# Score and value matmuls woven into one another, and matmuls that run on weights already loaded

## The chip, the cores and the metric

The kernel runs on one core of one Trainium2 chip. Its time is the device time of one execution in microseconds (us); the figure given is the median of several executions, and one more execution is profiled. TensorE (PE in the profile) does the matmuls; a weight load (LDWEIGHTS, PEld) puts the stationary operand into its array, and a matmul streams the other operand through. VectorE (DVE) and ScalarE (ACT) read the results, which stand in eight banks of PSUM, GpSimd (POOL) does some sums, and SyncE (SP) issues most DMAs.

## The reference

Two attention blocks read the same x of 2048 x 1024 (bfloat16) and are mixed by a gate per row. A is linear attention, B a local one over 8 positions, 2 apart, back from each row's own. Both have 32 heads of 32.

```python
x = A_x
g = sigmoid((x * gate_w).sum(-1, keepdims=True))

# A: linear attention
q, k, v = split(x @ A_wqkv)
phi = lambda t: where(t > 0, t + 1, exp(t)) + 1e-6
kv = einsum("bhsd,bhse->bhde", phi(k), v)
z = phi(k).sum over s
a = (phi(q) @ kv) / (phi(q) . z + 1e-6) @ A_wo

# B: position s sees s, s-2, ..., s-14
q, k, v = split(x @ B_wqkv)
logits = (q . k[s - 2 w]) / sqrt(32), masked where s - 2 w < 0
b = (softmax(logits) @ v[s - 2 w]) @ B_wo

out = g * a + (1 - g) * b
```

## The kernel before

Rows are reordered so that even positions come first and odd ones second: B's window is then 8 neighbours within one half. There are 16 tiles of 128 rows; xT holds x transposed, tile by tile. The program is a list of operations, each with an engine, a cost, what it reads and writes, and a function that emits its instructions (`P.op`). A planner (`Prog.schedule`) runs through that list with the costs, gives each engine its order, and lets free operations go to VectorE or ScalarE, whichever the plan has free first; PSUM banks come from pools, and the plan is made six times, each time with the banks' release times of the one before. Semaphores are put where an operation needs another engine's result. An operation of TensorE is one unit: its waits stand ahead of its first instruction, its signal on its last.

The stages on TensorE, in order:

1. Fifty small matmuls on constant ones (L1399, `WARM`), 156 columns each, while the first data comes.
2. B's values (L1363 by `group`): for each tile of x and each half (512 columns) of the weights eight matmuls of 128x512 add up in one bank; a move (L1390, L1391, `vst`) takes it out, and a DMA stores it in HBM (`vB_hbm`). The list `steps` sets the order: in a block of four tiles first the four with the first half, then the four with the second. Some steps carry an early load of later weights (`early`).
3. B's keys and queries (kT, qT; L1363), 64 groups of eight matmuls.
4. A's keys with phi (L1363), then the product of x and those keys (pk, xn; L1707). Every fifth group or so a burst of B's attention stands between them (`fill` and `burst`).
5. A's state (L1685), queries of A (kT, xT; L1363), folds of the state into the output weights (L1733), a flag of one column (L1621, `all_ok`) that says whether the fast path is valid, and the output products (L1778), 16 tiles by two halves, with each tile's normalized queries transposed into aT by DMA (L1763).

A burst has two parts. The scores (L1513): for each of 8 chunks four matmuls of 64x64 weights and 114 columns, one in each quadrant of the array. The values (L1537) of the burst before: for each of 16 head pairs four matmuls of 64x57 weights (the exponentials E) and 33 columns (v). There are 18 fills; the first burst has scores alone, the last values alone, and 17 have both. Before the change a burst emits all scores, then all values:

```python
            def fn(e):
                last = s_fn(e) if s_fn else None
                return v_fn(e) if v_fn else last
```

ScalarE's exponential (L1518) and VectorE's division (L1548, L1549) wait for the burst's signal. In all stages each matmul comes with its own weight load.

Of the kernel before, what the change touches and what calls it, by code (L numbers as in the profile page):

```python
# [1119 lines left out]
def build_kernel(nc, A_x, A_wqkv, A_wo, B_x, B_wqkv, B_wo, gate_w, out):  # L1120
    del B_x
    S = A_x.shape[1]
# [59 lines left out]
    banks = [Bank(i) for i in range(8)]  # L1182
# [14 lines left out]
    ws = [SB([128, 8, 1024], BF16, "w%d" % i) for i in range(4)]  # L1197
# [62 lines left out]
    def plan(seen):  # L1260
# [97 lines left out]

        def group(bank, lhs, rhs, reads, lo=0, hi=8):
            def fn(e):  # L1360
                last = None
                for dc in range(lo, hi):
                    last = e.matmul(bank.ap(), lhs(dc), rhs(dc), start=(dc == 0), stop=(dc == 7))  # L1363
                return last
            return P.op("pe", fn, (hi - lo) * mm(512), reads=reads, writes=[bank.iv])
# [32 lines left out]
        for i in range(WARM):  # L1398
            P.op("pe", lambda e: e.matmul(banks[7].ap(0, 156), one(128), one(156), start=True, stop=True), 0.13, writes=[banks[7].iv], prio=-1)  # L1399
# [4 lines left out]
        steps = []  # L1404
        for b in range(NT // 4):
            for half in range(2):
                if b == 0:
                    cuts = [(0, 4), (4, 6), (6, 8)] if half == 0 else [(0, 2), (2, 4), (4, 6), (6, 8)]
                    steps += [[(i, half, lo, hi) for i in range(2)] for lo, hi in cuts]
                    steps += [[(2, half, 0, 8)], [(3, half, 0, 8)]]  # L1410
                else:
                    steps += [[(4 * b + i, half, 0, 8)] for i in range(4)]
# [71 lines left out]
        def burst(s_fn, reads, cost):  # L1484
# [13 lines left out]
        def fill(e_, qs, nq, offs):  # L1498
# [10 lines left out]
            def s_fn(e):  # L1509
                for c in range(8):  # L1510
# [4 lines left out]
                return last  # L1515
# [13 lines left out]
            def v_fn(e):  # L1529
                for i in range(16):  # L1530
# [8 lines left out]
                return last  # L1539
# [365 lines left out]
```

## Time and profile before

| | |
|---|---|
| median of 3 runs | 479.21 us (479.09 to 479.43) |
| the profiled execution's own time | 479.6 us |
| its span | 477.9 us |
| granted TensorE clock, mean | 0.998 |
| TensorE busy | 468.0 us, 3988 matmuls in the records, 4035 weight loads |
| VectorE busy | 316.5 us |
| ScalarE busy | 130.0 us |

The span reaches from the first to the last instruction of the program; the execution's time is 1.7 us longer. Some matmul records are missing from the trace, so distances between matmuls that are twice the usual one are a missing record and no pause. A matmul's record is longer than its share of the time, since matmuls overlap: the distance from one start to the next is what it costs. The engine names are those above; in a group's row stand the line, the engine, the operation, what it writes and reads, the shape, the count, then busy time and mean length, then the idle time ahead of it.

### The profile page before, as it was taken

The page shows a single profiled execution, that of the slowest core. Times are in us where ns is not written, and L with a number is a line of the kernel's source. Part 1 is how long each engine was busy: PE and PEld are TensorE (multiplying, and loading weights), DVE is VectorE, ACT ScalarE, POOL GpSimd, SP SyncE. Part 2 cuts the span into 40 slices and gives each one's busy share as a digit, 9 for nine tenths or more (in the row PEclk, how much of TensorE's full clock was granted, in tenths as well). Part 3 has the DMA queues.
Part 4 walks back from the last instruction along what each step waited for, and adds up shares of the span by engine and source line. Part 5 has one row for each costly group of instructions (what it writes and reads, how often), then busy time and mean ns, then how long its engine had stood idle before and what let it go on. Part 6 is the DMA issues. An engine that isn't in the chain of part 4 may idle for free.

```text
span 477.9 us, 9322 instructions
## 1 busy us (share of the span) xinstructions
PE 468.0 (98%) x3988; PEld 226.1 (47%) x4035; DVE 316.5 (66%) x555; ACT 130.0 (27%) x174; POOL 40.2 (8%) x39
## 2 busy tenths in 40 slices
PE   9999999999999999999999999999999999999996
PEld 6444444444445444454445445544444444444444
DVE  2121276799877788878865465599987777777512
ACT  1112121112243535555543423153211111111000
POOL 3000000000000000000068551100000000000000
PEclk9999999999999999999999999999999999999999
DMA  9999995132211253354325876771241111421111
GB/s 234 229 214 315 355 363 153 59 118 67 67 37 51 67 167 85 80 158 124 77 71 154 182 166 128 152 207 45 68 88 45 44 46 50 73 55 45 46 44 48
DMA packets 94969, 57.07 MB, mean 119 GB/s; under 512 B 55240, under 2 KB 88392, under 8 KB 94920
## 3 DMA queue, kind: packets, MB, share of 16 engines
q1 hardware_dynamic: 94088, 55.61, 43.6%
q10 hardware_dynamic: 832, 0.79, 0.7%
q8 instruction: 33, 0.54, 0.5%
q14 instruction: 16, 0.13, 0.1%
HBM read 30.56 MB, written 12.72 MB: 91 GB/s over the span
## 4 chain that ended last, share of the span: by engine, by line
PE 98%; issue 1%; DVE 0%
PE ps_all L1363 58%; PE ps_all L1778 23%; PE ps_all L1707 11%; PE ps_all L1513 2%; PE ps_all L1537 2%; PE ps_all L1399 1%; PE ps_all L1685 0%; PE ps_all L1733 0%; DVE o L1393 0%; PE ps_all L1621 0%
## 5 line engine op out<-in xcount | busy, mean ns | idle before, releaser
L1363 PE MATMUL ps_all<-w,xT 128*128 128x512 bf16 x500 | 110.2, 379 | 1.3 <-issue 0.8
L1363 PE MATMUL ps_all<-xT,w 128*128 128x512 bf16 x500 | 110.2, 379 | 1.2 <-issue 0.8
L1363 PEld LDWEIGHTS ps_all<-xT,w 128*128 128x128 bf16 x512 | 49.6, 98 | 59.3
L1363 PEld LDWEIGHTS ps_all<-w,xT 128*128 128x128 bf16 x512 | 49.6, 98 | 58.9
L1369 ACT ACTIVATE e<-ps_all 128x512 bf16<-128x512 f32 x64 | 38.2, 598 | 123.4 <-PE ps_all L1363 122.1
L1778 PE MATMUL ps_all<-w,qT 128*128 128x512 bf16 (+1 forms) x256 | 59.7, 372 | 0.4
L1778 PE MATMUL ps_all<-kT,aT 128*128 128x512 bf16 (+1 forms) x258 | 59.9, 372 | 0.3
L1363 PE MATMUL ps_all<-kT,xT 128*128 128x512 bf16 x254 | 57.5, 379 | 0.3 <-issue 0.3
L1707 PE MATMUL ps_all<-pk,xn 128*128 128x512 bf16 x249 | 55.0, 379 | 1.1 <-issue 1.1
L1390 DVE CAST vst<-ps_all 128x512 bf16<-128x512 f32 x16 | 11.1, 694 | 44.7 <-PE ps_all L1363 44.7
L1778 PEld LDWEIGHTS ps_all<-kT,aT 128*128 128x128 bf16 x264 | 25.8, 98 | 29.5
L1778 PEld LDWEIGHTS ps_all<-w,qT 128*128 128x128 bf16 x264 | 25.8, 98 | 29.4
L1393 DVE TENSOR_SCALAR o<-ps_all,gm 128x512 bf16<-128x512 f32 (+1 forms) x28 | 20.5, 732 | 28.5 <-PE ps_all L1778 28.5
L1363 PEld LDWEIGHTS ps_all<-kT,xT 128*128 128x128 bf16 x256 | 24.7, 98 | 30.0 <-DVE pn L1758 0.2
L1707 PEld LDWEIGHTS ps_all<-pk,xn 128*128 128x128 bf16 x256 | 24.5, 98 | 28.8
L1370 DVE TENSOR_SCALAR e<-e 128x512 bf16<-128x512 bf16 x64 | 18.8, 294 | 28.1 <-ACT e L1369 27.6
L1518 ACT ACTIVATE E<-ps_all 128x1824 bf16<-128x1824 f32 (+1 forms) x18 | 30.4, 1688 | 21.0 <-PE ps_all L1537 19.4
L1671 POOL TENSOR_TENSOR zacc<-zacc,pk 128x1024 f32<-128x1024 f32 x15 | 32.8, 2188 | 12.1 <-DVE E L1523 11.2
L1549 DVE TENSOR_TENSOR ao<-ps_all,rs 128x896 bf16<-128x896 f32 (+1 forms) x36 | 24.5, 683 | 0.2
L1391 ACT ACTIVATE kT<-ps_all 128x512 bf16<-128x512 f32 x25 | 14.4, 598 | 34.7 <-PE ps_all L1363 34.7
L1391 ACT ACTIVATE vst<-ps_all 128x512 bf16<-128x512 f32 x16 | 9.6, 600 | 48.9 <-PE ps_all L1363 48.9
L1372 DVE SCALAR_TENSOR_TENSOR p<-ps_all,e 128x512 bf16<-128x512 f32 x32 | 22.0, 689 | 0.8
(65 smaller groups left out, 347.0 us busy)
## 6 DMA issues: line engine op xcount, KB each, us to landing
v<-vB_hbm SPq DMA_DIRECT2D x36, 132.0 KB, 3.0
vB_hbm<-vst SPq DMA_DIRECT2D x32, 132.0 KB, 5.2
w<-in_B_wqkv_dram SPq DMA_DIRECT2D x4, 1024.0 KB, 8.9
xt<-in_A_x_dram SPq DMA_DIRECT2D x16, 256.0 KB, 4.8
w<-in_A_wqkv_dram SPq DMA_DIRECT2D x4, 1024.0 KB, 9.4
xn<-in_A_x_dram SPq DMA_DIRECT2D x8, 512.0 KB, 5.0
out_dram<-o SPq DMA_DIRECT2D x15, 256.0 KB, 2.0
oB_hbm<-ao SPq DMA_DIRECT2D x32, 114.0 KB
```

The lines of the kernel that those rows point to most:

```text
L1363: last = e.matmul(bank.ap(), lhs(dc), rhs(dc), start=(dc == 0), stop=(dc == 7))
L1369: P.op("act", lambda e: e.activation(e_[:, :], bank.ap(), ACT.Exp), act(512), reads=[bank.iv], writes=[e_.all()])
L1370: P.op("dve", lambda e: e.tensor_scalar(e_[:, :], e_[:, :], 1.0, 1e-6, op0=ALU.min, op1=ALU.add), 0.25, reads=[e_.all()], writes=[e_.all()])
L1372: P.op("dve", lambda e: e.scalar_tensor_tensor(out=dst, in0=bank.ap(), scalar=0.0, in1=e_[:, :], op0=ALU.max, op1=ALU.add), dps(512), read ...
L1390: fd = lambda e: e.tensor_copy(dst, src())
L1391: fa = lambda e: e.activation(dst, src(), ACT.Copy)
L1393: fd = lambda e: e.tensor_scalar(dst, src(), scale, None, op0=ALU.mult)
L1518: P.op("act", lambda e: e.activation(E[:, 0:32 * nq].rearrange("p (j q) -> p j q", j=4), ps[:, 4:8, 0:8 * nq], ACT.Exp), act(32 * nq), rea ...
L1549: P.op("dve", lambda e, i0=i0, i1=i1, src=src: e.tensor_tensor(o_[:, :, i0:i1, :], src(0, 32), rs[:, :, i0:i1, None].to_broadcast([128, 2, ...
L1671: P.op("pool", lambda e, t=t: e.tensor_tensor(zacc[:, :], zacc[:, :], pkS[:, t, :], ALU.add), 2.2, reads=[src, zacc.all()], writes=[zacc.a ...
L1707: last = e.matmul(bank.ap(), tl[:, t, cs:cs + 128], pkS[:, t, r * 512:(r + 1) * 512], start=(t == 0), stop=(t == NT - 1))
L1778: last = e.matmul(bank.ap(0, f1 - f0), lh[:, k, t * 128:(t + 1) * 128], w[:, k, f0:f1], start=(first and k == 0), stop=(not first and k == 7))
```

## The change

Four edits.

- A burst is woven: after every group of four score matmuls come two groups of four value matmuls of the burst before. What it waits for and its one signal stay.
- In tiles 4 to 15 of B's values both halves of the weights are done together: for each of the eight chunks of x one load, a matmul into one bank, and a second matmul on the weights that are there into another bank. Each such pair is one operation of sixteen matmuls. The order of steps changes with it: the tiles come one after another, each with both halves.
- Of the fifty warm matmuls only the first loads its weights.
- The flag's matmul is listed after the first output tile instead of ahead of it.

12 x 8 and 49 make 145 loads fewer.

```diff
+        def same(e, out, lhs, rhs, start, stop):
+            return e.add_instruction(mybir.InstMatmult(name=nc.get_next_instruction_name(), engine=mybir.EngineType.PE, ins=[e.lower_ap(rhs), e.lower_ap(lhs)], outs=[e.lower_ap(out)],
+                                                       start_tensor_calc=start, stop_tensor_calc=stop, tile_size=(128, 128), tile_position=(0, 0), ldweights=False))
+
+        def two(bs, lhs, rhs, reads):
+            def fn(e):
+                for dc in range(8):
+                    e.matmul(bs[0].ap(), lhs(dc), rhs[0](dc), start=(dc == 0), stop=(dc == 7))
+                    last = same(e, bs[1].ap(), lhs(dc), rhs[1](dc), dc == 0, dc == 7)
+                return last
+            return P.op("pe", fn, 16 * mm(512), reads=reads, writes=[b.iv for b in bs])
...
-            P.op("pe", lambda e: e.matmul(banks[7].ap(0, 156), one(128), one(156), start=True, stop=True), 0.13, writes=[banks[7].iv], prio=-1)
+            P.op("pe", lambda e, i=i: same(e, banks[7].ap(0, 156), one(128), one(156), True, True) if i else e.matmul(banks[7].ap(0, 156), one(128), one(156), start=True, stop=True),
+                 0.13, writes=[banks[7].iv], prio=-1)
...
-                    steps += [[(4 * b + i, half, 0, 8)] for i in range(4)]
+                    steps += [[(4 * b + 2 * half + i, h, 0, 8) for h in range(2)] for i in range(2)]
...
-            if lo == 0:
+            if lo == 0 and (t, half) not in open_:
                 open_[t, half] = main.next()
...
-            o = group(bank, xs, w, [xr, ws[0].part((lo, hi), (half * 512, half * 512 + 512))], lo, hi)
+            if t < 4:
+                o = group(bank, xs, w, [xr, ws[0].part((lo, hi), (half * 512, half * 512 + 512))], lo, hi)
+            elif half == 0:
+                open_[t, 1] = main.next()
+                o = two([bank, open_[t, 1]], xs, [w, w_half(0, 1)[0]], [xr, ws[0].all()])
...
             def fn(e):
-                last = s_fn(e) if s_fn else None
-                return v_fn(e) if v_fn else last
+                S, V = [list(f) if f else [] for f in (s_fn, v_fn)]
+                for i in range(8):
+                    for f in S[i:i + 1] + V[2 * i:2 * i + 2]:
+                        last = f(e)
+                return last
...
-        flag_op = all_ok()
         for t in range(NT):
             if t + 2 < NT:
                 scaled(t + 2)
             output(t)
+            if t == 0:
+                flag_op = all_ok()
```

`s_fn` and `v_fn` become lists of 8 and 16 functions, one for each group of four matmuls.

TensorE around a burst with both parts, before: xT with w_5 and w_6 are keys and queries, qx with kT the scores, v with E the values.

```order
L1363 MATMUL ps_all<-xT_49,w_5_53 128x512 x16
L1513 MATMUL ps_all<-qx_82,kT_51 64x114 x32
L1537 MATMUL ps_all<-v_38_86,E_81 57x33 x64
L1363 MATMUL ps_all<-xT_49,w_6_54 128x512 x16
L1363 MATMUL ps_all<-xT_49,w_5_53 128x512 x16
```

The same burst now, its first part, on TensorE; L1375 is `group`, L1533 the scores, L1560 the values.

```order
L1375 MATMUL ps_all<-xT_49,w_5_53 128x512 x16
L1533 MATMUL ps_all<-qx_82,kT_51 64x114 x4
L1560 MATMUL ps_all<-v_38_86,E_81 57x33 x8
L1533 MATMUL ps_all<-qx_82,kT_51 64x114 x4
L1560 MATMUL ps_all<-v_38_86,E_81 57x33 x8
```

The 32 and the 64 matmuls have become eight rounds of 4 and 8; what stands before and after the burst is the same.

TensorE from the start of the program, now: L1411 is the one warm matmul with a load, L1360 is `same`, L1366 the first matmul of a pair; w_4 is slot 0 with the value weights. Before, the same stretch was two rows, 50 warm matmuls (L1399) and 256 value matmuls (L1363).

```order
L1411 MATMUL ps_all<-const-bfloat16-1.0 128x156
L1360 MATMUL ps_all<-const-bfloat16-1.0 128x156 x49
L1375 MATMUL ps_all<-w_4_52,xT_49 128x512 x64
L1366 MATMUL ps_all<-w_4_52,xT_49 128x512
L1360 MATMUL ps_all<-w_4_52,xT_49 128x512
```

The first four tiles, 64 matmuls, are as they were; from the fifth tile on each second matmul has no load, and two banks fill at once.

TensorE around the flag (okp), before; w_4 with qT and kT with aT are the two halves of an output sum, kT with kvT a fold, kT with xT a query of A.

```order
L1733 MATMUL ps_all<-kT_51,kvT_66 32x512 x16
L1621 MATMUL ps_all<-okp_73,const-bfloat16-1.0 128x1
L1778 MATMUL ps_all<-w_4_52,qT_50 128x512 x16
L1778 MATMUL ps_all<-kT_51,aT_57 128x512 x16
L1363 MATMUL ps_all<-kT_51,xT_49 128x512 x16
```

And now, the same place on TensorE.

```order
L1759 MATMUL ps_all<-kT_51,kvT_66 32x512 x16
L1804 MATMUL ps_all<-w_4_52,qT_50 128x512 x8
L1804 MATMUL ps_all<-kT_51,aT_57 128x512 x8
L1804 MATMUL ps_all<-w_4_52,qT_50 128x512 x8
L1647 MATMUL ps_all<-okp_73,const-bfloat16-1.0 128x1
L1375 MATMUL ps_all<-kT_51,xT_49 128x512 x8
L1804 MATMUL ps_all<-kT_51,aT_57 128x512 x8
L1375 MATMUL ps_all<-kT_51,xT_49 128x512 x8
```

The first product with aT stands 8 big matmuls behind the fold instead of 16, and the flag 24 behind it.

More of the change, by code (lines that the diff above doesn't have):

```diff
@@ L1507, in fill, with scores, fn @@
                 spread(e_, qs, nq, offs)
-            def s_fn(e):
-                for c in range(8):
+            def scores(c):
+                def fn(e):
                     for h in range(2):
@@ L1514, in s_fn @@
                                             qx[64 * g:64 * g + 64, :, c, h * nq:(h + 1) * nq], start=True, stop=True, tile_position=(64 * g, 64 * h))
-                return last
+                    return last
+                return fn
+            s_fn = [scores(c) for c in range(8)]
             burst(s_fn, [kT.part((0, 8), (t0 + k0[0], t0 + k0[1] + 64)), qx.all()], 0.4)
@@ L1527, in fill, with values, fn @@
                 after(3, lambda f=todo[0]: spread(*f, behind=[[o for o in P.ops if o.eng == "pe"][-1]]))
-            def v_fn(e):
-                for i in range(16):
+            def values(i):
+                def fn(e):
                     for h in range(2):
@@ L1538, in v_fn @@
                                             vt[64 * h:64 * h + 64, hd * 33:hd * 33 + 33], start=True, stop=True, tile_position=(64 * h, 64 * g))
-                return last
+                    return last
+                return fn
+            v_fn = [values(i) for i in range(16)]
             def results():
```

## The prediction

> **What bounds the kernel now.** First the page's busy row and its chain of waits.
>
> ```profile
> span 477.9 us, 9322 instructions
> PE 468.0 (98%) x3988; PEld 226.1 (47%) x4035; DVE 316.5 (66%) x555; ACT 130.0 (27%) x174; POOL 40.2 (8%) x39
> PE 98%; issue 1%; DVE 0%
> PE ps_all L1363 58%; PE ps_all L1778 23%; PE ps_all L1707 11%; PE ps_all L1513 2%; PE ps_all L1537 2%; PE ps_all L1399 1%; PE ps_all L1685 0%; PE ps_all L1733 0%; DVE o L1393 0%; PE ps_all L1621 0%
> ```
>
> The chain is TensorE (PE) from end to end; nothing else holds 1%. So the time falls only by what the matmuls' own sequence gets shorter, and rises by any wait put into it. Next the groups by line, shapes kept apart, for TensorE and its weight loads (count | busy us, mean ns of one).
>
> ```profile
> L1363 PE MATMUL ps_all<-xT,w 128*128 128x512 bf16 x500 | 110.2, 379 | 1.2 <-issue 0.8
> L1778 PE MATMUL ps_all<-w,qT 128*128 128x256 bf16 x16 | 2.1, 272 | 0.0
> L1537 PE MATMUL ps_all<-v,E 64*57 64x33 bf16 x1024 | 10.8, 180 | 0.0
> L1513 PE MATMUL ps_all<-qx,kT 64*64 64x114 bf16 x512 | 9.6, 212 | 0.0
> L1399 PE MATMUL ps_all<-const-bfloat16-1.0 128*128 128x156 bf16 x50 | 5.6, 301 | 0.8 <-PEq L1890 0.8
> L1685 PE MATMUL ps_all<-mT,w 128*64 128x64 bf16 x128 | 2.2, 196 | 0.0
> L1537 PEld LDWEIGHTS ps_all<-v,E 64*57 64x57 bf16 (+1 forms) x1152 | 11.1, 102 | 0.4 <-issue 0.4
> ```
>
> Matmuls overlap, so a mean is no price; the price is the distance from start to start. I read it off the timeline of TensorE around two bursts (start, length, name, count).
>
> ```profile
> 134.50 0.38 PE L1363 MATMUL ps_all<-xT,w 128*128 128x512 bf16 x1
> 134.81 0.60 PE L1513 MATMUL ps_all<-qx,kT 64*64 64x114 bf16 x32
> 135.25 0.67 PE L1537 MATMUL ps_all<-v,E 64*57 64x33 bf16 x64
> 136.08 8.58 PE L1363 MATMUL ps_all<-xT,w 128*128 128x512 bf16 x39 [0.16 <-issue]
> 144.59 0.60 PE L1513 MATMUL ps_all<-qx,kT 64*64 64x114 bf16 x32
> ```
>
> A big matmul: 39 in 8.58 us, the last 0.379 long, so (8.58 - 0.379) / 38 = 0.216 us apart, each with its own weight load. A column costs (379 - 272) / 256 = 0.418 ns by the two means, so 512 columns stream for 214 ns: the load in front of each adds at most 2 ns. It runs under the matmul ahead of it. A burst takes 0.44 us for its scores (32 matmuls, eight groups of four quadrants) and from 135.25 to 135.25 + 0.67 - 0.18 = 135.74 until its last value matmul starts: 0.49 us for 16 groups. The turn from full tiles into the burst costs 134.81 - 134.50 - 0.216 = 0.09 us.
>
> **The bursts.** A value matmul streams only 33 columns, 14 ns, yet a group of four takes 0.49 / 16 = 31 ns. Two views of 10 ns each, at the start and at the end of the value part, show how many are in flight:
>
> ```profile
> 135.42:135.43 0.01, 0.01 (x27) 0.01 (x13) 1.00 0.00 0
> 135.64:135.65 0.01, 0.01 (x23) 0.01 (x13) 1.00 0.00 0
> ```
>
> A record lasts about 180 ns and the view 10, so 27 in 190 ns are 28 ns a group, 23 are 33 ns. I read it so: at first a group waits for its weights (57 columns at 0.418 are 24 ns, and some 4), later it is the issue of 192 / 23 = 8.3 ns a pair of load and matmul that sets the pace, once what was queued under the scores is used up. A score group takes (0.44 - 0.03) / 8 = 51 ns, where 0.03 is the first group's load, which nothing hides; 114 columns stream for 48, so it waits for its own stream and leaves the issue idle for a third of the time.
>
> Woven, a trio is one score group and two value groups. Score to value: 51 ns, as before, since the value weights load under the score stream. Value to value: 28. Value to score: not in the trace; the score weights are 64 columns. The nearest row is the state product, L1685, 64 weight columns in groups of two: (2.2 - 0.196) / 64 = 31 ns. I take 31, so a trio is 110 ns. Its twelve pairs need 12 x 8.3 = 100 ns of issue, so issue no longer ends it. The burst from first to last start: 0.03 + 7 x 0.110 + 0.051 + 0.028 + 0.01 (inside the last group) = 0.89 us against 135.74 - 134.81 = 0.93. So 0.04 us a burst, and 17 bursts have both parts: **0.68 us less**. Bounds: if value to score goes at 27 and value to value at 27, the trio is 105 and the burst 0.85, 0.08 a burst, 1.3 us in all. On the other side, scores visit the quadrants rows first, values columns first, so at each turn the second and third of four swap; a place in a group is about 3 ns (four starts in 8 to 10), two turns a trio, 8 x 6 = 48 ns: a burst 8 ns longer than now, 0.1 us more in all. Between them I keep 0.68, since the state row is nearest in what it loads. ScalarE's exponential waits for the burst's last matmul before as after, since the burst gives one signal, at its end.
>
> The Trainium skill, TensorE: Matmul & The Clock Gate, The mechanism, speaks against the weave: a weight load runs under matmuls in flight only where its row group differs. Both kinds use both halves of the rows, so by it each load would be bared in either order and the weave would give nothing. Here 135.25 less the last score group's start, 134.81 + 0.03 + 7 x 0.051 = 135.20, is 0.05, with no load bared: the trace disagrees for that turn; the turn back no run shows yet.
>
> **The paired values.** For tiles 4 to 15 a load of xT serves two matmuls into two banks: 12 x 8 = 96 loads fewer. They ran under 214 ns of streaming, so the loads themselves give nothing. What may go is the 2 to 2.5 ns over the stream in the second matmul: 96 x 2.5 = 0.24 us at most, 0 at least. I take 0, as the same excess stands over 256 columns (8 in 1.04 us of the next row, (1.04 - 0.272) / 7 = 110 against 107), so it looks like a price of a matmul.
>
> ```profile
> 471.55 1.04 PE L1778 MATMUL ps_all<-w,qT 128*128 128x256 bf16 x8
> 58.31 0.69 DVE L1390 CAST vst<-ps_all 128x512 bf16<-128x512 f32 x1 [2.76 <-PE ps_all L1363]
> ```
>
> The Trainium skill, same page, "Wait — 56ns, not 53.3ns?", calls about 2.5 ns a fixed cost per matmul; by that the sum stays at 0, otherwise it is 0.24 more. No matmul here is without a load, so the trace can't tell.
>
> The order of the tiles costs nothing where three covers hold. Banks: a pair now frees two of seven at once, 3.45 us apart; two casts of 0.69 on one engine need 1.4, and VectorE stood idle 2.76 ahead of each (row above). If that cover went, TensorE would wait up to 0.7 a pair. Tiles of x: tile 4b + i was needed 1.73 i after its block began and is now needed 3.45 i after, never earlier. Weights: each early load hangs on a step that comes at the same place or earlier, and SyncE's queue issues it behind the same x tiles.
>
> **The warm matmuls.** TensorE's first microseconds, matmuls and loads, with the counts by stretch and x's first tile (queue row, issue, and us to landing):
>
> ```profile
> 0.84 5.63 PE L1399 MATMUL ps_all<-const-bfloat16-1.0 128*128 128x156 bf16 x50 [0.84 <-PEq L1890]
> 0.84:5.10 4.26, 4.25 (x34) 4.26 (x35) 1.00 0.75 205
> 6.24 0.38 PEld L1363 LDWEIGHTS ps_all<-w,xT 128*128 128x128 bf16 x3
> 0.81 2.80 SPq L1336 DMA_TRANSPOSE xT<-in_A_x_dram  x2
> xT<-in_A_x_dram SPq DMA_TRANSPOSE x1, 5.3
> ```
>
> 34 start by 5.10, 0.13 apart: 156 columns at half the later pace, 2 x 65, so there the load is hidden. The last 16 take 6.24 - 5.10 = 1.1 us, 0.071 apart, against 65 + 2.5: 16 x 0.0035 = 0.05 us that the missing loads can give. The first real load follows at once at 6.24, and x's tile lands at 0.81 + 5.3 = 6.1, so there is room for most of it, not for more. I take 0.05, bounds 0 and 0.05.
>
> **The flag.** The one-column matmul moves behind the first output tile, which splits that tile's products and the next query.
>
> ```profile
> 324.36 0.43 PE L1733 MATMUL ps_all<-kT,kvT 32*32 32x512 bf16 x16
> 324.73 0.18 PE L1621 MATMUL ps_all<-okp,const-bfloat16-1.0 128*128 128x1 bf16 x1
> 324.98 3.40 PE L1778 MATMUL ps_all<-w,qT 128*128 128x512 bf16 x15
> 317.95 9.90 SPq L1763 DMA_TRANSPOSE aT<-pn  x2
> aT<-pn SPq DMA_TRANSPOSE x16, 2.8
> ```
>
> From 324.73 to 324.98 are 0.25, one big matmul (0.216; its record is missing) and 0.04 for the flag; it pays that anywhere. Now aT is wanted 8 big matmuls behind the fold instead of 16, at 324.77 + 1.73 = 326.5; it was issued at 317.95 and lands 2.8 later. Cost 0; if the queue were 6 us late, TensorE would wait from there.
>
> **The sum.** 0.68 + 0 + 0.05 + 0 = 0.73 us off the profiled execution: 479.6 becomes 478.9. The median of the runs shown is 479.21, 0.4 lower than that execution; the terms are differences, so **478.5 us**, 0.15% less. 0.2%, 0.96 us here, is about the least that a measurement of this kernel can tell from no change, so the likeliest case lies just inside it.
>
> **The rivals.** *All terms at their better ends*: 1.3 + 0.24 + 0.05 = 1.6 off, 477.6; 0.96 is reached by a burst 0.054 shorter, or by 0.04 with the 0.24. For it speaks that value loads start at 28 ns; against it the 31 of the state row. Chance of over 0.2%: 0.30. *The weave gives nothing*, because the turn from value to score bares a load or the swapped quadrants stall: 0.05 off at most, 479.2; for it that this turn is nowhere in the trace. 0.15. The Trainium skill's rule on row groups, above, would end here. *The turn costs as much as entering a burst*, 0.09 us, seven times in 17 bursts: 119 x 0.09 = 10.7 us, less 0.73, 489.2. It decides from 0.68 / 119 = 6 ns a turn on, and is slower by 0.2% from (0.73 + 0.96) / 119 = 14 ns on. Against it: both kinds are 64-row tiles, and the turn from score to value is free. 0.10 with milder forms. *The second matmul of a pair holds back the next load*: bared as at a burst's entry, 96 x 0.09 = 8.6 us, 487; against it, a load needs only the matmul ahead to have begun, and 214 ns of it hide it. 0.02. *The loads are still issued*: then the counts of loads stay and 478.5 stands but for 0.05; it has no chance of its own.
>
> **How the numbers follow.** The likeliest case, 0.43, is within 0.2% and so is the empty weave, 0.15: same 0.58. Faster 0.30, slower 0.10 + 0.02. The range runs from the better ends, 477.6, to the empty weave with its swapped quadrants and the spread of runs (479.09 to 479.43), 479.5; it leaves out the slow rivals and little else.
>
> **What would show it.** In the changed profile: loads 145 fewer; a burst from first score to last value start near 0.89 us, and the big matmul after it at the same distance as now; the first real load at 6.19; pairs at 0.216 each, or 0.2145 where the excess goes. Wrong would be a burst over 0.93, any idle time ahead of a value pair, or a wait for aT at 326.5.

## The result, and the profile after

The kernel after the change takes 477.99 us in the median of 7 runs (477.32 to 479.33), against 479.43 of 7 runs of the kernel before on the same chip (478.99 to 479.87). The ratio is 0.9968, 95% interval 0.9954 to 0.9983: 0.3% faster, 1.4 us by the medians. The time lies inside the predicted range. My likeliest case said a gain of 0.15% and the estimate is 0.32%; so it lies in the class "faster by over 0.2%", to which I gave 0.30, though the interval reaches down to 0.17%.

The profiled execution of the kernel after took 477.52 us, 2.1 less than that of before. First the page's rows:

```profile
span 475.7 us, 9166 instructions
PE 467.0 (98%) x3988; PEld 210.7 (44%) x3890; DVE 313.0 (66%) x554; ACT 130.1 (27%) x175; POOL 40.2 (8%) x39
PE 93%; DVE 3%; DMA 2%; issue 1%; POOL 0%; ACT 0%; DVEq 0%
PE ps_all L1375 46%; PE ps_all L1804 23%; PE ps_all L1733 11%; PE ps_all L1360 6%; PE ps_all L1366 4%; PE ps_all L1533 2%; PE ps_all L1560 1%; DMA z_hbm<-zc 1%; DMA zr<-z_hbm 1%; DVE p L1384 1%; DVE prod L1779 0%; DVE den L1780 0%; POOL zb L1687 0%; DVE kT L1402 0%; DVE pn L1784 0%
```

4035 weight loads have become 3890, the 145 fewer. The chain is not TensorE from end to end any more: it leaves TensorE for the denominators' sums, which are stored (z_hbm<-zc), loaded back (zr<-z_hbm), copied (zb) and multiplied by VectorE (prod). That is a path that the prediction does not name. The same two stretches of the timeline as before, a burst and what follows it:

```profile
134.49 0.24 PE L1533 MATMUL ps_all<-qx,kT 64*64 64x114 bf16 x4
134.56 0.21 PE L1560 MATMUL ps_all<-v,E 64*57 64x33 bf16 x8
134.62 0.22 PE L1533 MATMUL ps_all<-qx,kT 64*64 64x114 bf16 x4
...
135.30 0.22 PE L1533 MATMUL ps_all<-qx,kT 64*64 64x114 bf16 x4
135.35 0.21 PE L1560 MATMUL ps_all<-v,E 64*57 64x33 bf16 x8
135.72 8.58 PE L1375 MATMUL ps_all<-xT,w 128*128 128x512 bf16 x39 [0.16 <-issue]
```

The weave is there, four scores and eight values by turns. From the first score's start to the last value's (135.35 + 0.21 - 0.18) are 0.89 us, 0.93 before. The second to the eighth trio: 135.30 - 134.62 = 0.68 over six of them, 0.113 each. Read to the nanosecond the burst goes from 0.925 to 0.896 us, and with what stands around it from 9.777 to 9.744 us a period: 0.033 us a burst, 0.56 for 17.

Pairs, from the timeline of the kernel after:

```profile
28.00 0.38 PE L1366 MATMUL ps_all<-w,xT 128*128 128x512 bf16 x1
28.21 0.38 PE L1360 MATMUL ps_all<-w,xT 128*128 128x512 bf16 x1
...
33.83 0.38 PE L1360 MATMUL ps_all<-w,xT 128*128 128x512 bf16 x1
```

27 steps in 33.83 - 28.00 = 5.83 us, 0.216 each, with a load (L1366) and without (L1360) alike. The start:

```profile
0.84 0.29 PE L1411 MATMUL ps_all<-const-bfloat16-1.0 128*128 128x156 bf16 x1 [0.84 <-PEq L1917]
0.93 5.14 PE L1360 MATMUL ps_all<-const-bfloat16-1.0 128*128 128x156 bf16 x49
5.96 0.99 PEld L1375 LDWEIGHTS ps_all<-w,xT 128*128 128x128 bf16 x6 [5.04 <-DMA w<-in_B_wqkv_dram]
```

The first real load comes at 5.96, 0.28 earlier than before. In two more profiles of the same kernel it comes at 6.08 and 6.91, so this is one execution's luck and no term of the change.

Then the stage where the chain leaves TensorE. The timeline of before and of after, GpSimd's copy and VectorE's product behind it (start, length, idle time ahead):

```profile
308.15 2.06 POOL L1661 COPY zb<-zr 128x1024 bf16<-128x1024 bf16 x1 [19.74 <-DMA zr<-z_hbm]
310.31 1.23 DVE L1753 TENSOR_TENSOR prod<-p,zb 128x1024 f32<-128x1024 bf16 x1 [0.48 <-POOL zb L1661]
```

```profile
308.55 2.01 POOL L1687 COPY zb<-zr 128x1024 bf16<-128x1024 bf16 x1 [21.00 <-DMA zr<-z_hbm]
310.67 1.23 DVE L1779 TENSOR_TENSOR prod<-p,zb 128x1024 f32<-128x1024 bf16 x1 [1.72 <-POOL zb L1687]
323.61 0.44 PE L1759 MATMUL ps_all<-kT,kvT 32*32 32x512 bf16 x16
324.44 1.67 PE L1804 MATMUL ps_all<-w,qT 128*128 128x512 bf16 x7 [0.39 <-DVE p L1384]
```

At the last burst TensorE is 0.9 us ahead of before (0.28 from the start, 0.61 from the matmuls behind it); the copy is not, it starts 0.4 later than before. Its path sets out as early: the first transfer that transposes the sums is issued 8.70 us ahead of the last burst's last value load, 8.73 before. But it lands 4.86 us after its issue, 4.20 before, and the store of the sums takes 5.18 us, 4.39 before. VectorE waits 1.72 in place of 0.48, its later work shifts, and TensorE, which has no wait here before, stands idle ahead of L1804; by distances from start to start the stage from 306 to 326 us loses 0.38.

Last the end. The DMA view of before between 473.95 and 478 us, and of after between 473.45 and 476, from the last output store on (code loads are on the queue named instruction; a store's last figure is us from issue to landing):

```profile
q1 hardware_dynamic: 153, 0.07, 6.3%
q8 instruction: 1, 0.02, 2.1%
out_dram<-o SPq DMA_DIRECT2D x1, 64.0 KB, 3.4
```

```profile
q1 hardware_dynamic: 153, 0.07, 10.3%
out_dram<-o SPq DMA_DIRECT2D x1, 64.0 KB, 1.7
```

The same store lands 3.4 us after its issue before and 1.7 after. These views count a packet by its start: before, a 16 KB block of code starts behind the store's issue at 474.01; after, the block starts ahead of the issue at 473.49. The queue's row in two narrow windows, of before between 474.9 and 475.1 us and of after between 472.45 and 472.55:

```profile
q8 instruction: 1, 0.02, 42.5%
```

```profile
q8 instruction: 1, 0.02, 90.6%
```

In the trace's records TensorE's branch behind its last matmul takes 2.37 us before and 0.40 after. From the last matmul's start to the end of the span there are 4.67 us before and 3.01 after, 1.66 less.

So the 2.18 us between the two spans are 0.28 at the start (luck), 0.61 up to the last burst (0.56 of it the weave), minus 0.38 in the fold stage, and 1.66 at the end. The first term is chance, the second was predicted, the last two were not in the prediction's sum; the third will turn out to be chance as well.

### The profile page after: what moved, and what is told of

Read it like the earlier page. It is cut to its first block, busy times and chain, and to the rows that moved or that the text cites. A ratio compares the mean times of both kernels' runs of the same rounds, so it can differ in the third digit from the quotient of the medians.

```text
span 475.7 us, 9166 instructions
## 1 busy us (share of the span) xinstructions
PE 467.0 (98%) x3988; PEld 210.7 (44%) x3890; DVE 313.0 (66%) x554; ACT 130.1 (27%) x175; POOL 40.2 (8%) x39
## 4 chain that ended last, share of the span: by engine, by line
PE 93%; DVE 3%; DMA 2%; issue 1%; POOL 0%; ACT 0%; DVEq 0%
PE ps_all L1375 46%; PE ps_all L1804 23%; PE ps_all L1733 11%; PE ps_all L1360 6%; PE ps_all L1366 4%; PE ps_all L1533 2%; PE ps_all L1560 1%; DMA z_hbm<-zc 1%; DMA zr<-z_hbm 1%; DVE p L1384 1%; DVE prod L1779 0%; DVE den L1780 0%; POOL zb L1687 0%; DVE kT L1402 0%; DVE pn L1784 0%
## 5 line engine op out<-in xcount | busy, mean ns | idle before, releaser
L1375 PE MATMUL ps_all<-xT,w 128*128 128x512 bf16 x500 | 110.2, 379 | 1.2 <-issue 0.8
L1375 PEld LDWEIGHTS ps_all<-xT,w 128*128 128x128 bf16 x512 | 49.6, 98 | 59.5 <-issue 0.3
L1375 PE MATMUL ps_all<-w,xT 128*128 128x512 bf16 x312 | 69.0, 379 | 1.1 <-DVE e L1382 1.0
L1804 PE MATMUL ps_all<-kT,aT 128*128 128x512 bf16 (+1 forms) x259 | 60.2, 372 | 0.3
L1804 PE MATMUL ps_all<-w,qT 128*128 128x512 bf16 (+1 forms) x255 | 59.7, 372 | 0.8 <-DVE p L1384 0.4
L1375 PE MATMUL ps_all<-kT,xT 128*128 128x512 bf16 x254 | 57.6, 379 | 0.3 <-issue 0.2
L1375 PEld LDWEIGHTS ps_all<-w,xT 128*128 128x128 bf16 x320 | 30.6, 98 | 41.5 <-DMA w<-in_B_wqkv_dram 5.5
L1804 PEld LDWEIGHTS ps_all<-w,qT 128*128 128x128 bf16 x264 | 25.7, 98 | 29.9 <-DVE p L1384 0.5
L1804 PEld LDWEIGHTS ps_all<-kT,aT 128*128 128x128 bf16 x264 | 25.8, 98 | 29.4
L1375 PEld LDWEIGHTS ps_all<-kT,xT 128*128 128x128 bf16 x256 | 24.6, 98 | 29.9 <-issue 0.5
L1360 PE MATMUL ps_all<-w,xT 128*128 128x512 bf16 x96 | 36.4, 379 | 0.2
L1366 PE MATMUL ps_all<-w,xT 128*128 128x512 bf16 x92 | 34.9, 379 | 0.0
```

The costliest lines, as they stand in the source:

```text
L1360: return e.add_instruction(mybir.InstMatmult(name=nc.get_next_instruction_name(), engine=mybir.EngineType.PE, ins=[e.lower_ap(rhs), e.lowe ...
L1366: e.matmul(bs[0].ap(), lhs(dc), rhs[0](dc), start=(dc == 0), stop=(dc == 7))
L1804: last = e.matmul(bank.ap(0, f1 - f0), lh[:, k, t * 128:(t + 1) * 128], w[:, k, f0:f1], start=(first and k == 0), stop=(not first and k == 7))
```

## Experiments

Eleven kernels ran, each in five rounds beside the kernel before. What each left is in this table. "Matmuls" is from the first real weight load to the last matmul's start, so that the start's luck is out of it. "Landing" is of the first transposing transfer of the sums, from its issue. "Lag" is from the last burst's last value load to the start of GpSimd's copy of the returned sums (in z_twice, of the copy that is used). "Lost" is what the time from that load to the last matmul exceeds 175.17 us, the least seen. "End" is from the last matmul's start to the span's end. All in us, worked out from starts in the traces.

| kernel | loads fewer | matmuls | landing | lag | lost | end | ratio to before (95%) |
|---|---|---|---|---|---|---|---|
| before | 0 | 466.95 | 4.20 | 10.13 | 0.00 | 4.67 | |
| before_again | 0 | 466.99 | 4.24 | 10.52 | 0.05 | 3.93 | 1.0029 (1.0003 to 1.0054) |
| weave_only | 0 | 467.71 | 5.87 | 11.80 | 1.32 | 3.95 | 0.9996 (0.9983 to 1.0010) |
| loads_back | 0 | 466.44 | 5.12 | 10.81 | 0.00 | 4.25 | 0.9983 (0.9975 to 0.9992) |
| warm_only | 49 | 467.13 | 4.16 | 10.65 | 0.19 | 3.02 | 0.9980 (0.9968 to 0.9992) |
| pairs_only | 96 | 468.73 | 5.94 | 12.15 | 1.67 | 3.02 | 0.9982 (0.9969 to 0.9995) |
| after | 145 | 466.71 | 4.86 | 11.43 | 0.38 | 3.01 | 0.9968 (0.9954 to 0.9983) |
| after_again | 145 | 466.39 | 4.12 | 10.66 | 0.00 | 3.01 | 0.9973 (0.9960 to 0.9985) |
| after_third | 145 | 466.38 | 4.51 | 10.95 | 0.00 | 3.01 | 0.9974 (0.9958 to 0.9991) |
| flag_back | 145 | 467.78 | 5.26 | 11.89 | 1.41 | 2.90 | 0.9990 (0.9978 to 1.0002) |
| z_early | 145 | 467.26 | 3.20 | 4.88 | 0.00 | 2.90 | 0.9958 (0.9943 to 0.9972) |
| z_due | 145 | 467.47 | 3.23 | 11.98 | 0.92 | 2.90 | 0.9981 (0.9963 to 0.9998) |
| z_twice | 145 | 468.25 | 4.53 | 12.88 | 1.84 | 3.08 | 1.0031 (1.0011 to 1.0052) |

In z_early the last burst stands one group of eight matmuls, 1.73 us, later in TensorE's order; its 173.44 us behind that burst are 175.17 with them.

**The kernel before a second time.** No edit: how far do two builds of one kernel differ?

> The kernel before, unchanged, once more. Page theory (TensorE's code comes in loads of 16 KB on queue 8, 256 instructions each, and one that falls on the last output store delays it): code loads again near 471 and 475 us, the last store lands about 3.4 us after its issue, the branch near 472 takes over 2 us, span 477.5 to 478.2. Chance theory (the last landing and the clock's rise are luck of one execution): the last store lands anywhere from 1.7 to 3.4 us after its issue. Time ratio 1.000, with its interval within 0.002 of it.

It came out 0.29% slower than the kernel before, with an interval that just leaves out 1, which was not expected. Two of its twelve runs took 484.3 and 485.3 us; by the medians, 479.98 against 479.52, it is 0.10%. So two builds can differ by much of what is to be explained here, and small terms have to be read from distances in the traces, not from the times. Its matmuls take the same 467.0 us within 0.05; its end has the same two code loads after 470 us, a branch of 2.01 us and a last store that lands 2.6 us after its issue, and is 3.93.

**The kernel after twice more.** No edit either.

> The kernel after the change, unedited, built a second time under another name. Theory A (the end of the kernel is set by where TensorE's code blocks are fetched): its last code block ahead of the end is fetched by 473 us, the branch at its end takes about 0.4 us, and 3.0 us lie between the last matmul's start and the end, as in its first profile; the rise of the clock, which the program doesn't set, falls anywhere between 4.3 and 6.6 us; ratio 0.996 to 0.998. Theory B (both ends of the kernel are chance): branch, end and start differ from its first profile, the end by up to 1.7 us; ratio 0.996 to 1.000.

> The kernel after the change, unedited, beside the two others on the same chip. Theory A (its gain is the bursts' 0.57 us and the end's 0.9 to 1.7 us, less what the late sums take): 466.3 to 466.8 us from the first real load to the last matmul, 3.0 us behind it; ratio 0.996 to 0.998. Theory B (both are chance of one build): a last part of 3.9 us or more, or the bursts' 0.57 us gone; ratio 0.998 to 1.001.

The end is 3.01 both times, as in the first profile, the bursts' gain is there, and both ratios lie beside the first, 0.9973 and 0.9974. The loss in the fold stage is not: 0.00 both times against 0.38. So end and weave belong to the program, that loss to the execution: the first transposing transfer landed after 4.12 and 4.51 us, against 4.86. The timeline of TensorE in the second build:

```profile
323.64 0.43 PE L1759 MATMUL ps_all<-kT,kvT 32*32 32x512 bf16 x16
324.01 1.90 PE L1804 MATMUL ps_all<-w,qT 128*128 128x512 bf16 x8
```

No idle time stands ahead of L1804, and the fold follows what was before it at once.

**The weave alone.** The kernel before with the woven order and nothing else:

```diff
-                last = s_fn(e) if s_fn else None
-                return v_fn(e) if v_fn else last
+                S, V = [list(f) if f else [] for f in (s_fn, v_fn)]
+                for i in range(8):
+                    for f in S[i:i + 1] + V[2 * i:2 * i + 2]:
+                        last = f(e)
```

> The kernel before with the woven bursts alone; no instruction fewer. Page theory: 17 bursts by 0.033 us, 0.57 us less, and the tail as in the kernel before (last store 3.4 us after its issue): ratio 0.9988. Work theory (the whole measured 1.4 us comes from shorter work on TensorE): bursts save most of it, ratio 0.997. Burst from first score to last value start 0.896 us in both.

No change that can be told from noise, 0.9996; the interval holds the first theory's 0.9988 and not the second's 0.997. Up to the last burst TensorE is 0.56 us ahead, and then it loses 1.32. The timeline of TensorE where it does:

```profile
324.21 0.44 PE L1754 MATMUL ps_all<-kT,kvT 32*32 32x512 bf16 x16 [0.45 <-DVE kT L1402]
324.81 0.18 PE L1642 MATMUL ps_all<-okp,const-bfloat16-1.0 128*128 128x1 bf16 x1 [0.16 <-DVE p L1384]
325.64 2.11 PE L1799 MATMUL ps_all<-w,qT 128*128 128x512 bf16 x9 [0.65 <-DVE den L1776]
```

Three waits for VectorE in 1.5 us: ahead of a fold, of the flag's matmul at its old place, and of the first product of A's output. In this profile the transposing transfer took 5.87 us to land. The DMA view of before (289 to 290 us) and of this kernel (288.6 to 289 us):

```profile
zt<-zb SPq DMA_TRANSPOSE x1, 4.2
```

```profile
zt<-zb SPq DMA_TRANSPOSE x1, 5.9
```

Its end has two code loads and is 3.95, as in the kernel before built again.

**Warm matmuls alone, pairs alone, and all loads back.** The kernel before with only the 49 warm loads taken out; with only the 96 of the pairs taken out; and the kernel after with all 145 put in again, its order kept:

```diff
-                    last = same(e, bs[1].ap(), lhs(dc), rhs[1](dc), dc == 0, dc == 7)
+                    last = e.matmul(bs[1].ap(), lhs(dc), rhs[1](dc), start=(dc == 0), stop=(dc == 7))
...
-            P.op("pe", lambda e, i=i: same(e, banks[7].ap(0, 156), one(128), one(156), True, True) if i else e.matmul(banks[7].ap(0, 156), one(128), one(156), start=True, stop=True),
-                 0.13, writes=[banks[7].iv], prio=-1)
+            P.op("pe", lambda e: e.matmul(banks[7].ap(0, 156), one(128), one(156), start=True, stop=True), 0.13, writes=[banks[7].iv], prio=-1)
```

> The kernel before with the 49 warm loads left out alone: 49 instructions fewer. Page theory: TensorE's code loads move 49 instructions, about 5 us, later, so none falls on the last store, which lands 1.5 to 1.8 us after its issue: 1.7 us less plus 0 to 0.3 at the start, ratio 0.996. Work theory: 0.05 us less by shorter warm matmuls, 0.3 if the missing loads make the clock rise earlier, ratio 0.9994 to 0.9999. The clock's rise (row before: 5.1 us, row after: 4.3 us): near 4.3 if the loads delay it, anywhere if it is luck.

> The kernel before with the pairs of the later values alone: 96 weight loads fewer, no weave, no change to the warm-up, the flag at its old place. Theory A (fewer instructions move the code blocks away from the end): the matmuls up to the folds take the same time within 0.05 us counted from the first real weight load (a pair takes 0.216 us for each matmul, with the load or without), but the branch at the end takes about 0.4 us in place of 2.0 to 2.4 and 3.0 us lie between the last matmul's start and the end in place of 3.9 to 4.7; ratio 0.996 to 0.998. Theory B (the work decides): the pairs bring nothing and the end stays as it was; ratio 1.000.

> The kernel after with all 145 loads put back: pairs in the new order, each matmul with its own load, warm matmuls with theirs, bursts woven, flag at its new place. Page theory: the code loads fall as in the kernel before, the last store lands 3.4 us after its issue: 0.57 us less by the weave, 0 to 0.4 lost at the wait at 323 us, ratio 0.9988 to 0.9996. Work theory: loads are hidden, so nothing is lost against the kernel after, ratio 0.997. Pairs at 0.216 us a matmul in both.

These three settle the end. The DMA view from 470 us to the end, code loads, of the kernel before and of the kernel with the loads back:

```profile
q8 instruction: 2, 0.03, 2.1%
```

```profile
q8 instruction: 2, 0.03, 1.9%
```

and the same row of the kernel with the pairs alone, with its last store behind it (from 476.2 us on):

```profile
q8 instruction: 1, 0.02, 1.0%
...
out_dram<-o SPq DMA_DIRECT2D x1, 64.0 KB, 1.7
```

Each of the four programs with all loads has two code loads after 470 us and an end of 3.9 to 4.7; each of the nine with 49, 96 or 145 fewer has one, and 2.9 to 3.1. Taking the loads out of the warm-up or out of the pairs does the same, and putting them back undoes it: what counts at the end is how many instructions stand ahead of it, not what they do.

The trace's packet records show how. In all thirteen profiles TensorE's last block of code starts 0.72 to 0.73 us after its last branch ends, and the span ends 0.48 us after the last store lands. In the four with all loads the block before the last is still arriving when the branch begins (471.32 to 472.81 in the kernel before, the branch at 471.90), the branch takes 1.9 to 2.4 us, and the last block falls on the last store: 120 of the store's 128 packets of 512 bytes start within 0.32 us, the other 8 only as the block ends (474.84 to 475.16, then from 476.33 on, with the block from 474.99 to 476.35). In the other nine the block before the last is through 3.3 us or more ahead of the branch, the branch takes 0.40, and the last block is through before that store's first packet. There it holds up the store ahead of the last, which takes 2.8 to 3.4 us to land, and that costs nothing. That the long branch waits for the arriving block is likely but not shown.

Of the ratios, that of the warm loads alone fits neither theory (0.9980, where 0.996 or 0.9994 to 0.9999 was expected); the intervals of the other two hold values of the first theory and none of the second. The pairs themselves bring nothing: from the first real load to the last of B's value matmuls it takes 55.11 us in the kernel before and 55.11 with the pairs alone. The kernel with the pairs alone lost 1.67 in the fold stage of its profile, so its 0.9982 is its shorter end less part of such losses.

The Trainium skill, Runtime: NRT & Kernel Launch, Instruction fetch mechanics, says that code is refilled in blocks of 16 KiB, 256 instructions, ahead of use, that crossing a block is mostly hidden, and that a taken branch whose target is not in the window must wait for a fetch. The blocks agree with the trace: 33 packets make 0.54 MB on that queue, 16 KB each. "Mostly hidden" holds inside the kernel before, where the distance from burst to burst stays at 9.76 to 9.78 us while blocks are loaded, and not at its end, where a block is worth 0.9 to 1.7 us. Whether the branch there waits for its target no run shows.

**The flag at its old place.** The kernel after with that one edit taken back:

```diff
+        flag_op = all_ok()
...
-            if t == 0:
-                flag_op = all_ok()
```

> The changed kernel with the flag of the masks taken at its old place, behind the loop, in place of behind the first fold. Theory A (the old place puts a matmul and a bank behind work of VectorE that is late once the bursts are shorter): TensorE waits 0.5 to 1 us more between 320 and 327 us than with the flag at its new place, as in the kernel with the weave alone, where the waits came to 1.27 us; last matmul 0.5 to 1 us later, ratio 0.998 to 1.000. Theory B (the place of the flag costs nothing, and the kernel with the weave alone lost its time by the sums that come back late): within 0.1 us of the changed kernel, ratio 0.997.

It loses 1.41 us in the fold stage, more than the 0.5 to 1 us expected, and the ratio, 0.9990, is where the first theory had it. The timeline of TensorE:

```profile
324.73 0.44 PE L1759 MATMUL ps_all<-kT,kvT 32*32 32x512 bf16 x16 [0.50 <-DVE kT L1402]
325.33 0.18 PE L1647 MATMUL ps_all<-okp,const-bfloat16-1.0 128*128 128x1 bf16 x1 [0.16 <-DVE p L1384]
325.93 1.90 PE L1804 MATMUL ps_all<-w,qT 128*128 128x512 bf16 x8 [0.42 <-DVE kT L1402]
```

The three waits of the weave alone, at the same instructions. But its copy also came late, 11.89 behind the last value load against 10.66 to 11.43 in the kernel after, so the place of the flag is not the whole of it. The table shows how the two go together. With the flag at its old place, lag less lost is 10.46 to 10.48 us in the five profiles that lost anything. At its new place it is 11.05 in the first profile of the kernel after, and lags of 10.66, 10.81 and 10.95 lost nothing. So TensorE loses one for one what the copy is later than a limit, and the flag's new place moves the limit by 0.58. That the copy is the cause, and not only late together with something else, needed a kernel that delays it alone.

**The copy made twice.** The kernel after with GpSimd's copy made first into a buffer that nobody reads, then into its own. Every engine keeps its order.

```diff
+            def spread(e):
+                for to in (zz, zb):
+                    last = e.tensor_copy(to[:, :].rearrange("q (c p) -> q c p", c=8), zr[:, :].rearrange("q (p c) -> q c p", c=8))
+                return last
-            P.op("pool", lambda e: e.tensor_copy(zb[:, :].rearrange("q (c p) -> q c p", c=8), zr[:, :].rearrange("q (p c) -> q c p", c=8)), 1.4, reads=[zr.all()], writes=[zb.all()])
+            P.op("pool", spread, 1.4, reads=[zr.all()], writes=[zb.all()])
```

> The changed kernel with GpSimd's copy of the returned sums made twice, first into a buffer that nobody reads, then into its own: the product of VectorE that reads it can start one copy, 2.02 us, later; the order of every engine is that of the changed kernel. Theory A (TensorE loses, one for one, what the copy comes later than a limit): in the ten profiles so far the time from the last burst's last value load to the last matmul is 175.17 us plus what the copy's start lies later than 10.47 us behind that load with the flag at its old place, and than about 11.06 us with the flag at its new place. A copy that comes 2.02 us later, from a start 10.66 to 11.43 us behind that load, costs 1.6 to 2.4 us: 176.8 to 177.6 us from the last value load to the last matmul; ratio to the kernel before 0.0035 to 0.005 above that of the changed kernel. Theory B (the copy's place is only a companion of the waits, which come from something else): 175.2 to 175.6 us as in the two profiles of the changed kernel, the same ratio.

From the last value load to the last matmul it takes 177.01 us, inside the first theory's 176.8 to 177.6; lag less lost is 11.04. The timeline, the two copies and then TensorE:

```profile
308.37 2.01 POOL L1690 COPY zz<-zr 128x1024 bf16<-128x1024 bf16 x1 [20.51 <-DMA zr<-z_hbm]
310.31 2.03 POOL L1690 COPY zb<-zr 128x1024 bf16<-128x1024 bf16 x1
...
316.62 0.44 PE L1764 MATMUL ps_all<-kT,kvT 32*32 32x512 bf16 x16 [0.62 <-DVE kT L1403]
317.55 3.40 PE L1376 MATMUL ps_all<-kT,xT 128*128 128x512 bf16 x15 [0.50 <-DVE kT L1403]
325.39 0.44 PE L1764 MATMUL ps_all<-kT,kvT 32*32 32x512 bf16 x16 [0.51 <-DVE kT L1403]
326.21 1.46 PE L1809 MATMUL ps_all<-w,qT 128*128 128x512 bf16 x6 [0.39 <-DVE p L1385]
```

Nothing but the copy was delayed, and the waits of the fold stage came, all for VectorE's casts and products that stand behind the product with the sums. The ratio is 0.0057 above that of the kernel after beside it, where 0.0035 to 0.005 was expected; the miss of 0.0007 is small beside the intervals, 0.0041 and 0.0033 wide, which do not meet. So the copy is the cause.

**The sums earlier.** All sixteen additions handed out four at a time in place of three, so that they end some 8 us sooner, in two forms. The two lines of z_add alone are z_early, all three are z_due:

```diff
-        z_add(3)
+        z_add(4)
...
-                        z_add(3)
+                        z_add(4)
...
-                     writes=[zt.part((i, i + 1), (0, 8), (0, 128))], chan="zt%d" % i, lat=1.3, prio=51)
+                     writes=[zt.part((i, i + 1), (0, 8), (0, 128))], chan="zt%d" % i, lat=3.3, prio=51)
```

> The changed kernel with the 16 additions of the denominators handed out four by four instead of three by three, so that the last of them is queued some 3.8 us earlier (by the trace of the kernel after the change: at 284.6 in place of 288.4 us). Nothing else is edited. Theory A (the sums that leave for memory and come back are late for the folds, and take back part of what the bursts gained): the copy of the returned sums on GpSimd comes 3 to 4 us earlier, VectorE no longer waits 1.72 us ahead of its product, TensorE's waits of 0.14 us ahead of a fold of line 1759 and 0.23 us ahead of line 1804 go, and the last matmul comes 0.2 to 0.4 us earlier, counted from the first real weight load; ratio to the kernel before 0.9955 to 0.9965. Theory B (those waits of TensorE come from VectorE's own order, or from banks): the copy comes earlier, TensorE's last matmul stays within 0.1 us; ratio 0.997.

In z_early the copy starts at 304.95, 3.0 to 4.1 us sooner than in the three profiles of the kernel after, and all waits of the fold stage are gone, as the first theory had it. But the last matmul is 0.55 to 0.88 later and not earlier, since TensorE stood idle in the last burst. VectorE and TensorE there:

```profile
293.22 2.27 DVE L1682 TENSOR_REDUCE zs<-zt 128x16 f32<-128x2048 bf16 x1
295.62 1.08 DVE L1546 TENSOR_TENSOR E<-E,msk 128x1792 bf16<-128x1792 bf16 x1
...
298.71 0.65 PE L1560 MATMUL ps_all<-v,E 64*56 64x33 bf16 x61
300.05 0.22 PE L1560 MATMUL ps_all<-v,E 64*56 64x33 bf16 x3 [0.68 <-issue]
```

I first read this as the mask's product (L1546) coming late behind the reduction, and the next expectation says so. The rows deny it: the product ends at 296.70, the burst starts two us later, and the idle time stands among its own matmuls, with no wait shown and no block of code loaded between 294 and 307 us. Its cause stays open. The ratio, 0.9958 from five runs, is the lowest of all, but its interval overlaps those of the kernel after, and its profiled execution is slower than each of theirs; no gain is shown.

> The changed kernel with the additions of the denominators handed out four by four, as in the earlier run, and with the landing of the transposed sums put down at 3.3 us in the planner in place of 1.3, so that VectorE's reduction of them stands behind the mask of the last burst again, where the earlier run had it ahead and the last burst waited 0.76 us. Theory A (with the copy some 2 us earlier than in the changed kernel nothing of the fold stage waits, and the last burst doesn't either): last value load to last matmul 175.2 us, first real load to last matmul 466.3 to 466.5 us, 0 to 0.4 us under the changed kernel; ratio 0.0000 to 0.0008 below the changed kernel's. Theory B (an earlier chain brings another wait again): over 466.7 us, ratio at or above the changed kernel's.

This failed in another way: the transposed sums were there at 291.5, 4.9 us sooner than in the kernel after built again, and yet the copy started no earlier, at 309.29. VectorE and ScalarE show where the time went:

```profile
297.84 0.10 DVE L1683 TENSOR_TENSOR zc<-zs 128x8 bf16<-128x8 f32 x1
299.38 0.60 ACT L1403 ACTIVATE mT<-ps_all 128x512 bf16<-128x512 f32 x1 [3.57 <-PE ps_all L1733]
299.38 0.35 ACTq L1684 DMA_DIRECT2D z_hbm<-zc  x1
303.80 0.34 ACTq L1685 DMA_DIRECT2D zr<-z_hbm  x1
```

The sums are ready at 297.94, but ScalarE has to issue a cast of mT first that waits for TensorE until 299.38; the store behind it goes out at 299.38, as in the kernel after built again. The load back then took 5.4 us where the kernel after has 3.5 to 3.7. Lag less lost is 11.06, the limit once more. A better kernel would have to move the store off that queue; I did not try it.

## Why the prediction was right, and where it was not

**The weave: right, a sixth too large.** 0.68 us was forecast, 0.56 came. The trio was put at 110 ns and takes 112. By the starts in the trace the turn from value to score, for which I took the state product's 31, takes 29; value to value, put at 28, takes 27; score to value, put at 51 because it takes that before, takes 56 in the woven burst. So the turn that no trace had shown was cheap, and one taken as known was 5 ns too low; why, no run shows (the swapped quadrants may be in it). The rest is 0.93 read to hundredths, which is 0.925. The better end did not come, and the rival by which each turn costs as much as entering a burst is out. By the Trainium skill's rule on row groups, cited there, the weave would have given nothing; it gave 0.56 us, and the turn back costs 2 ns more than from value to value.

**The pairs: right.** 0 was taken of 0 to 0.24; 0.216 with and without a load, and the same 55.11 us for the stage. The excess over the stream belongs to the matmul, as the Trainium skill says in the section cited there. No bank was waited for.

**The warm matmuls: of no account.** 0.05 was forecast. The first real load's time varies from 5.96 to 6.91 in three profiles of one kernel, so 0.05 can't be seen.

**The flag: the wrong question.** "Cost 0" was right, and aT was never waited for. But I asked what its new place costs and not what its old place costs: up to 0.58 us wherever the copy comes later than 10.47 us behind the last value load. With the flag left where it was, the kernel with the weave alone lost in that stage of its profile more than the weave gave.

**The sum: two terms missing.** It went by TensorE's distances and took the rest of the execution as fixed. The end is not: 145 instructions fewer move the borders of the code blocks, so the last block no longer falls on the last store, and 0.9 to 1.7 us come off behind the last matmul. Nothing in the sum stood for that, though the last store's late landing was there to read. The other is the copy of the sums. Its path sets out with TensorE, woven or not: in the eleven profiles that don't move the additions, the first transposing transfer is issued 8.70 to 8.73 us ahead of the last value load, so the weave's gain does not make the copy late. But that transfer lands 4.1 to 5.9 us after its issue, without the weave (4.2 to 5.9) as with it (4.1 to 5.9). In the kernel before the copy starts 0.3 us inside its limit in one profile and 0.05 outside in the other, so there was next to no cover for a late landing, before as after. The forecast named the covers of the pairs and of aT, not this one. By the table the terms are 0.56 for the weave, 3.01 against 4.67 and 3.93 at the end, 1.3 in the mean, and minus 0.1 for the fold stage in the mean of three: 1.75 us, 0.37%, against 0.26 to 0.32% measured. So the range held by its better end, which I had built from other terms: the gain over 0.2% was given 0.30 for the weave's and the pairs' better bounds, and it came from the end. For the time this was luck; for the weave and the pairs it was not.

**Still open:** the idle 0.68 us in one burst of z_early, why the turn from score to value grows from 51 to 56 ns, why the transposing transfer lands so unevenly, and what sets the two long runs in the second build of the kernel before apart.

## What to carry to other kernels

Before pricing a gain on the engine that bounds, list what arrives there from a side path (here sums that go out to memory and back), with how much room each has left and how far its landings scatter from execution to execution; what comes later than that room turns into a wait, and an edit of the order, here of the flag's place, can move the limit. An edit that takes out instructions also moves the borders of the code blocks, so look at the last matmul to the end of the span by itself, before and after, and put the loads back in one run to see which part of the gain is the work and which the code's length. Where two builds of one kernel differ by as much as the change brings, compare distances inside the trace, and delay a suspect on purpose to see whether the loss follows it one for one.

## What the runs showed of the hardware

A 16 KB block of code that starts behind the last store's issue costs 0.9 to 1.7 us at the end: 8 of the store's 128 packets start only as the block ends, and the store lands 2.6 to 3.4 us after its issue in place of 1.6 to 1.8. TensorE's last branch takes 1.9 to 2.4 us where a block is still arriving as it begins, and 0.40 where none is. A matmul of 512 columns takes 0.216 us whether its weights are loaded ahead of it or there already. 2 KB of sums stored and 256 KB loaded back take 4.4 to 5.2 and 3.5 to 5.4 us, and a transposing transfer of the same 128x1024 tile lands 3.2 to 5.9 us after its issue in thirteen profiles, which is the larger part of what the fold stage loses or doesn't: in the eleven profiles that don't move the additions it scatters by 1.8 us and the copy's lag by 2.0.
